# A new order for all queues of a fused recurrent-gate and gated-convolution kernel

## The chip, the cores and the metric

The kernel runs on one core of a Trainium2 chip. A core has TensorE (PE in the profile; its weight loads are PEld), VectorE (DVE), ScalarE (ACT), GpSimd (POOL) and SyncE (SP), which here only issues transfers. Each takes its own instructions strictly in order and waits at an instruction until what it needs is there. The metric is the device time of one execution in microseconds (us); lower is better.

## The reference

Two layers, one behind the other, on `x` of 4 x 6336 x 256 in float32. The first is a gated linear recurrence, the second a gated unit whose gate is a causal convolution over five time steps.

```python
# first layer, c = 8
sig_r, sig_i = sigmoid(r_gate), sigmoid(i_gate)
a_t  = exp(c * sig_r * log(sigmoid(a_param)))
norm = sqrt(maximum(1 - a_t * a_t, 1e-6))
x_gated = norm * sig_i * x
h = a_t[:, t] * h + x_gated[:, t]            # over t; y[:, t] = h
# second layer, on y
gate = sigmoid(sum_k conv_w[k] * y shifted by 4 - k)
out  = (gate * (y @ w_val)) @ w_out
```

## The kernel before

The 25,344 rows (batch and time laid end to end) are cut into 51 windows, of 512 rows each but for two of 256 at the start and one of 256 at the end; 28 chunks hold one or two windows each. Windows 0, 1 and 2 are chunks 0, 1 and 2; chunk 3 holds windows 3 and 4, chunk 4 windows 5 and 6, and so on; windows 49 and 50 are chunks 26 and 27. Sigmoids are worked out as half of one plus a tangent (tanh), so that tanh and exp share one table of ACT.

The program is one list of words, `ORDER` (line 35 on): the loop at the end of the kernel (from `for word in ORDER.split()`) reads it word by word and calls the function that the word names, which issues its instructions. Nothing else orders them: each engine's queue is the sequence of its words in the list, and what waits for what across engines follows from the buffers. A word such as `tr.5.0@6,7` is operation `tr` on chunk 5, half 0, in banks 6 and 7 of the accumulation memory (PSUM). The operations:

| word | engine, line | on | what it does |
|---|---|---|---|
| `lr`, `li`, `lx` | SP L278 | window | load of r_gate, i_gate, x into a ring of 4 windows each (`rring`, `iring`, `xring`) |
| `ta`, `tb` | ACT L296, L299 | chunk | tangent of r, of i; frees the ring slots of `lr`, `li` |
| `tr` | PE L343 | chunk group, half | transposes of the tangent of r to channels by time |
| `ex` | ACT L359 | group, half | `a_t` by an exponential, from PSUM into `aring` |
| `sq`, `sa` | POOL L367, ACT L375 | chunk, half | `a_t` squared, into `ering` |
| `rt` | ACT L386 | batch of 1 to 3 chunks | the norm by a square root; needs another table than exp and tanh |
| `pp`, `up` | POOL L306, L318 | window | one plus the tangent of i, times x, into `uring` |
| `xp`, `uv` | PE L323, DVE L332 | window | the same product by another way, for windows 1, 2 and 6 |
| `nt`, `xg` | PE L401, DVE L408 | chunk | norm transposed back; times `uring` |
| `xt` | PE L417 | chunk | the product transposed to channels by time |
| `sc` | DVE L439 | chunk, half | the recurrence, a scan along time, into `yring`; the next chunk's scan starts from its last value |
| `cv`, `tg` | PE L451, ACT L458 | window | the convolution as 20 small matmuls, its tangent |
| `vl`, `gv` | PE L466, DVE L471 | window | `y @ w_val`; gate times value, into `tgring` |
| `ou` | PE L481 | window | times `w_out`, into PSUM |
| `cd` or `ca` | DVE L489 or ACT L491 | window | copy of the output from PSUM to `oring`, a ring of 4 windows |
| `st` | SP L502 | window | store of the output |

Words with `s_` set up constants (`s_wl` loads weights on SP, `s_wcast` casts them on POOL). Where a word needs ACT's other table, a table load (L518) goes ahead of it. Loads and stores share one queue, SP's: a store that waits for its copy holds up the loads behind it in the list. A load waits until its ring slot is free, so `lr.8` for the tangent that read window 4. A matmul into a bank waits until the bank's last reader is done.

Of the kernel before, what the change touches and what calls it, by code (L numbers as in the profile page):

```python
# [15 lines left out]
CHUNKS = [[256], [256], [512], [512, 512], [512, 512], [512, 512], [512, 512], [512, 512], [512, 512], [512, 512], [512,  # L16
    512], [512, 512], [512, 512], [512, 512], [512, 512], [512, 512], [512, 512], [512, 512], [512, 512], [512,
    512], [512, 512], [512, 512], [512, 512], [512, 512], [512, 512], [512, 512], [512], [256]]
BATCHES = [[0], [1], [2], [3, 4], [5, 6, 7], [8, 9, 10], [11, 12, 13], [14, 15, 16], [17, 18, 19], [20, 21, 22], [23, 24,
    25], [26, 27]]  # L20
# [11 lines left out]
GROUPS = [[0], [1], [2], [3, 4], [5, 6], [7, 8], [9, 10], [11], [12], [13, 14], [15, 16], [17, 18], [19, 20], [21], [22],  # L32
    [23, 24], [25], [26], [27]]
# [516 lines left out]
```

## Time and profile before

| what | us |
|---|---|
| time, median of 3 runs (lowest, highest) | 296.55 (295.05, 296.58) |
| span of the profiled execution | 294.6 |
| DVE busy: scans, 62 instructions | 106.2 |
| DVE busy: gates `gv`, 51 | 59.0 |
| DVE busy: copies `cd`, 33 | 38.3 |
| ACT busy: `ex`, 38 | 54.5 |
| ACT busy: `tg`, 51 | 49.7 |
| ACT busy: `ta`, 28, and `tb`, 28 | 47.8 and 48.0 |
| ACT busy: `rt`, 15 instructions | 44.7 |
| ACT busy: table loads, 18 | 23.1 |
| ACT busy: copies `ca`, 18 | 17.8 |
| a load or store of 512 KB, from issue to landing | 7.6 to 7.9 loads, 5.2 stores |

The span runs from the first to the last instruction of the profiled execution, and the time of a run is a little more. Busy times of engines overlap; a group's row gives its total and the mean of one instruction. The sum by engine is in the page's first part. The chain that ended last is put at 38% ACT, 23% transfers, 20% PE and 12% "issue", that is, time in which the engine on the chain waited for nothing that the profile shows.

### The profile page before, as it was taken

The numbers are of one execution on the slowest core, as the hardware profiler recorded it, in microseconds if no ns is written. First come the engines' busy times: TensorE is split into PE (matmuls) and PEld (weight loads), VectorE is DVE, ScalarE is ACT, GpSimd is POOL, SyncE is SP. The second block draws the span as 40 slices with busy tenths as digits, with TensorE's granted clock in tenths as the row PEclk, the third lists the DMA queues.
The fourth block names the chain that finished last, engine by engine and source line by source line (L and its number), as shares of the span: only waits on it lengthen the run. The fifth ranks groups of instructions, "written<-read, shape, count | busy, mean of one in ns | idle before, by whom it ended". The sixth has DMA issues, their size and how long they took to land.

```text
span 294.6 us, 6238 instructions
## 1 busy us (share of the span) xinstructions
PE 241.6 (82%) x2497; PEld 165.2 (56%) x2497; DVE 241.5 (82%) x198; ACT 277.3 (94%) x202; POOL 241.8 (82%) x161
## 2 busy tenths in 40 slices
PE   2263879778697899988969889989889998899993
PEld 1241556436464767666636647566648674767652
DVE  2000697867999899997999998999999999999981
ACT  6799999999999999999999899999999999999754
POOL 1559979999999799999997989999997999666200
PEclk9999999999999999997999999999999999999998
DMA  7999999999999999999988999999999999965336
GB/s 242 336 414 388 383 408 401 403 412 376 414 398 405 401 383 388 392 356 417 385 257 312 364 411 414 415 350 406 374 389 384 392 331 369 346 249 209 153 142 249
DMA packets 29994, 104.74 MB, mean 355 GB/s; under 512 B 3335, under 2 KB 3854, under 8 KB 29966
## 3 DMA queue, kind: packets, MB, share of 16 engines
q1 hardware_dynamic: 29952, 104.35, 92.5%
q8 instruction: 19, 0.31, 0.4%
q14 instruction: 9, 0.07, 0.1%
q10 hardware_dynamic: 14, 0.01, 0.0%
HBM read 78.39 MB, written 25.95 MB: 354 GB/s over the span
## 4 chain that ended last, share of the span: by engine, by line
ACT 38%; DMA 23%; PE 20%; issue 12%; DVE 4%; SPq 1%; ACTq 0%; DVEq 0%
DMA rring<-in_r_gate_dram 10%; DMA iring<-in_i_gate_dram 9%; ACT aring L359 7%; ACT tgring L458 7%; ACT taring L296 7%; ACT ering L386 6%; ACT tbring L299 6%; PE banks L466 5%; PE banks L481 4%; PE banks L451 4%; ACT L518 4%; DMA xring<-in_x_dram 4%; PE banks L401 2%; PE banks L417 2%; DVE tgring L471 2%
## 5 line engine op out<-in xcount | busy, mean ns | idle before, releaser
L439 DVE TENSOR_TENSOR_SCAN yring<-aring,yring,banks 128x1024 bf16<-128x1024 f32 (+5 forms) x54 | 106.2, 1991 | 2.1 <-PE banks L417 1.9
L318 POOL TENSOR_TENSOR uring<-tbring,xring 128x1024 bf16<-128x1024 bf16 (+1 forms) x48 | 100.8, 2117 | 8.2 <-DMA xring<-in_x_dram 4.8
L367 POOL TENSOR_TENSOR ering<-aring 128x1024 f32<-128x1024 f32 (+2 forms) x54 | 91.5, 1714 | 11.7 <-ACT aring L359 11.6
L451 PE MATMUL banks<-yring,diag 64*64 64x512 bf16 (+7 forms) x1080 | 62.2, 362 | 3.0 <-DVE yring L439 1.1
L471 DVE SCALAR_TENSOR_TENSOR tgring<-tgring,banks 128x1024 bf16<-128x1024 bf16 (+1 forms) x51 | 59.0, 1179 | 5.7 <-ACT tgring L458 3.6
L306 POOL TENSOR_SCALAR tbring<-tbring 128x1024 bf16<-128x1024 bf16 (+1 forms) x48 | 48.9, 1030 | 13.1 <-ACT tbring L299 11.3
L481 PE MATMUL banks<-wo,tgring 128*128 128x256 bf16 x396 | 51.2, 274 | 8.3 <-DVE tgring L471 7.5
L359 ACT ACTIVATE aring<-banks,khf 128x2048 f32<-128x2048 bf16 (+3 forms) x38 | 54.5, 1472 | 1.6 <-PE banks L343 1.5
L466 PE MATMUL banks<-yring,wv 128*128 128x512 bf16 (+4 forms) x216 | 51.1, 366 | 4.7 <-ACT tgring L458 2.2
L458 ACT ACTIVATE tgring<-banks 128x1024 bf16<-128x1024 f32 (+1 forms) x51 | 49.7, 1008 | 3.4 <-PE banks L451 3.3
L481 PEld LDWEIGHTS <-tgring 128*128 128x128 bf16 x396 | 41.5, 114 | 18.7 <-DVE tgring L471 13.6
L296 ACT ACTIVATE taring<-rring 128x2048 bf16<-128x2048 f32 (+2 forms) x28 | 47.8, 1721 | 1.9 <-DMA rring<-in_r_gate_dram 1.9
L299 ACT ACTIVATE tbring<-iring 128x2048 bf16<-128x2048 f32 (+2 forms) x28 | 48.0, 1720 | 0.6 <-DMA iring<-in_i_gate_dram 0.5
L386 ACT ACTIVATE ering<-ering 128x4096 bf16<-128x4096 f32 (+5 forms) x15 | 44.7, 3016 | 0.1
L451 PEld LDWEIGHTS <-diag 64*64 64x64 bf16 x1080 | 29.0, 106 | 26.8 <-issue 10.7
L408 DVE TENSOR_TENSOR uring<-banks,uring 128x2048 bf16<-128x2048 bf16 (+2 forms) x28 | 30.3, 1095 | 15.9 <-PE banks L401 13.4
L489 DVE COPY oring<-banks 128x1024 f32<-128x1024 f32 (+1 forms) x33 | 38.3, 1183 | 5.5 <-PE banks L481 5.1
L343 PE MATMUL banks<-ident_b,taring 128*128 128x128 bf16 x396 | 30.1, 230 | 15.1 <-ACT taring L296 10.4
L343 PEld LDWEIGHTS <-taring 128*128 128x128 bf16 x396 | 26.1, 103 | 21.1 <-ACT taring L296 12.0
L466 PEld LDWEIGHTS <-wv 128*128 128x128 bf16 x216 | 19.7, 98 | 26.2 <-issue 13.1
L401 PE MATMUL banks<-ident,ering 128*128 128x128 f32 x198 | 30.0, 297 | 5.3 <-ACT ering L386 2.9
L401 PEld LDWEIGHTS banks<-ident,ering 128*128 128x128 f32 x198 | 26.9, 208 | 11.2 <-ACT ering L386 5.6
(37 smaller groups left out, 126.0 us busy)
## 6 DMA issues: line engine op xcount, KB each, us to landing
rring<-in_r_gate_dram SPq DMA_DIRECT2D x48, 512.0 KB, 7.6
iring<-in_i_gate_dram SPq DMA_DIRECT2D x48, 512.0 KB, 7.6
xring<-in_x_dram SPq DMA_DIRECT2D x48, 512.0 KB, 7.9
out_dram<-oring SPq DMA_DIRECT2D x48, 512.0 KB, 5.2
rring<-in_r_gate_dram SPq DMA_DIRECT2D x3, 256.0 KB, 3.0
iring<-in_i_gate_dram SPq DMA_DIRECT2D x3, 256.0 KB, 3.2
xring<-in_x_dram SPq DMA_DIRECT2D x3, 256.0 KB, 6.4
out_dram<-oring SPq DMA_DIRECT2D x3, 256.0 KB, 5.7
```

The lines of the kernel that those rows point to most:

```text
L296: nc.scalar.activation(**tangent(c, taring, NTR, rring, NRI))
L299: nc.scalar.activation(**tangent(c, tbring, NTI, iring, NII))
L318: nc.gpsimd.tensor_tensor(out=u, in0=t1, in1=xt, op=ALU.mult)
L359: nc.scalar.activation(out=dst, in_=src, func=ACT.Exp, scale=khf[:, h:h + 1], bias=khf[:, h:h + 1])
L367: nc.gpsimd.tensor_tensor(out=e, in0=a, in1=a, op=ALU.mult)
L401: nc.tensor.transpose(out=bank[:, k:k + P], in_=ering[:, e + q:e + wins[w] // 2:nq], identity=ident[:])
L439: nc.vector.tensor_tensor_scan(out=yring[:, h, col:col + o1 - o0], data0=aring[:, h, a_at[c] + o0:a_at[c] + o1], data1=xT[:, o0:o1], initi ...
L451: nc.tensor.matmul(out=gp[oh * 64:oh * 64 + 64, h, a:b], lhsT=diag[half * 64:half * 64 + 64, h, k, :], rhs=yring[half * 64:half * 64 + 64, ...
L458: nc.scalar.activation(out=tgring[:, w % NTG, :, 0:wins[w]], in_=live.pop(("gp", w))[:, :, 0:wins[w]], func=ACT.Tanh, scale=0.5)
L466: nc.tensor.matmul(out=val[:, m, a:b], lhsT=wv[:, hk, m * P:(m + 1) * P], rhs=yring[:, hk, col:col + b - a], start=(hk == 0), stop=(hk == ...
L471: nc.vector.scalar_tensor_tensor(out=tgring[:, w % NTG, :, 0:wins[w]], in0=tgring[:, w % NTG, :, 0:wins[w]], scalar=1.0, in1=live.pop(("va ...
L481: nc.tensor.matmul(out=ops[:, j * D:(j + 1) * D], lhsT=gv[:, hk, j:wins[w]:J], rhs=wo[:, hk, :], start=(hk == 0), stop=(hk == H - 1))
```

## The change

Only `ORDER` differs; the lists of chunks, batches and groups are wrapped to other line lengths with the same contents, and all code behind the list stands one line lower. Both lists have 961 words, and they are the same words but for five: `ca.8`, `ca.23`, `ca.33`, `ca.34` and `ca.49` became `cd.8`, `cd.23`, `cd.33`, `cd.34` and `cd.49`. The sequence of every queue differs, and so do most bank numbers. Buffers, their sizes and the shapes of all instructions are as before. Table loads between `rt` and the other words number 18 in both.

Below are the start of the list and its end, from just ahead of `rt.10`, before and after.

```diff
-s_ident s_small s_kt s_diag lr.0 ta.0 lr.1 ta.1 li.0 tr.0.1@0 tb.0 pp.0 tr.0.0@1 ex.0.1 tr.1.0@2 tr.1.1@3 lr.2 ta.2
-ex.1.0 tr.2.1@0 ex.1.1 ex.2.1 tr.2.0@2 lr.3 lr.4 lr.5 ex.0.0 ta.3 lr.6 ta.4 li.1 tr.3.1@0,1 lx.1 tb.1 sq.2.1 sq.1.1
-sq.0.1 ex.2.0 li.2 tr.3.0@2,3 li.4 lx.0 li.3 tb.2 xp.1@4 sq.0.0 sq.1.0 sq.2.0 up.0 uv.1 lr.7 lr.8 ex.3.1 sq.4.1 ex.3.0
-sq.3.0 lr.9 lr.10 lx.2 lx.4 s_wl.2 lx.3 li.5 li.6 s_wl.1 tb.3 s_wl.3 s_wl.0 ta.5 lx.5 ta.6 lr.14 rt.0 xp.2@2,3 nt.0@4
-xg.0 xt.0@0,1 li.8 li.7 uv.2 rt.1 rt.2 nt.1@4 nt.2@5 xg.2 xg.1 pp.4 sq.3.1 sq.4.0 lx.6 rt.3 lr.11 tb.4 lr.12
-tr.5.0@6,7 ex.5.0 xt.1@5,4 li.9 lr.13 sc.0.0 sc.0.1 pp.3 up.4 lx.8 nt.3@2,3 xt.2@0,1 sc.1.0 li.10 up.3 sc.1.1 xg.3
-xt.3@2,3 tb.5 cv.1@4,5 sc.2.1 lx.7 sc.2.0 tg.1 cv.0@6,7 tg.0 tr.5.1@0,1 ex.5.1 s_wcast vl.1@4,5 sc.3.1 sc.3.0 xp.6@6,7
-vl.0@0,1 nt.4@2,3 li.12 pp.5 ta.7 lr.16 sq.5.0 sq.6.0 up.5 li.11 ta.8 pp.8 uv.6 tb.6 gv.0 ou.0.0@0 lr.15 cv.2@6,7 tg.2
...
-xg.22 ex.25.1 li.46 cv.38@6,7 tg.38 sa.25.1 tb.24 pp.45 xt.22@2,3 ou.36.0@0,1 cv.37@6,7 tg.37 st.34 st.33 st.35
-sc.21.0 cv.39@4,5 lx.43 tg.39 up.43 cd.36.0 vl.37@0,1 lx.46 sc.22.0 lx.45 gv.37 rt.10 vl.38@6,7 gv.38 ou.37.0@0,1
-ou.38.0@6,7 sc.22.1 cd.38.0 cv.40@4,5 cd.37.0 tg.40 li.48 vl.39@2,3 gv.39 st.36 nt.23@6,7 pp.46 up.45 up.46 li.47
-tb.25 pp.48 pp.47 lr.49 ta.26 lx.47 st.37 st.38 li.49 li.50 xg.23 vl.40@0,1 gv.40 nt.24@2,3 xg.24 xt.23@6,7 sc.23.1
-ou.39.0@4,5 ca.39.0 tr.27.0@0 tr.27.1@1 ex.27.1 ex.27.0 lx.50 lx.48 cv.42@2,3 up.47 tg.42 st.39 cv.41@4,5 tg.41
-sc.23.0 up.48 ou.40.0@0,1 ca.40.0 st.40 sa.27.1 vl.41@2,3 gv.41 vl.42@4,5 gv.42 tr.26.1@6 sq.27.0 tr.26.0@7 ex.26.0
-xt.24@0,1 sc.24.0 ex.26.1 sq.26.1 sc.24.1 tb.26 pp.49 sq.26.0 ou.41.0@2,3 ca.41.0 cv.43@4,5 cv.44@6,7 vl.43@2,3 tg.43
-ou.42.0@4,5 tg.44 rt.11 st.41 lx.49 nt.25@6,7 ca.42.0 gv.43 vl.44@0,1 xg.25 ou.43.0@2,3 xt.25@6,7 ca.43.0 gv.44
-cv.46@4,5 tb.27 tg.46 cv.45@2,3 tg.45 sc.25.1 sc.25.0 st.42 ou.44.0@0,1 ca.44.0 nt.26@7 st.43 st.44 up.49 xg.26
-vl.46@4,5 gv.46 vl.45@2,3 gv.45 cv.47@0,1 tg.47 ou.46.0@4,5 ca.46.0 xt.26@6,7 sc.26.0 ou.45.0@0,1 vl.47@2,3 ca.45.0
-st.45 nt.27@4 cv.48@5,6 tg.48 sc.26.1 cv.49@0,1 tg.49 gv.47 pp.50 up.50 xg.27 xt.27@5,4 sc.27.1 vl.49@2,3 ou.47.0@6,7
-ca.47.0 st.46 vl.48@0,1 gv.49 ou.49.0@2,3 ca.49.0 sc.27.0 st.47 cv.50@6,7 tg.50 gv.48 st.49 ou.48.0@0,1 ca.48.0 st.48
-vl.50@2,3 gv.50 ou.50.0@2 ca.50.0 st.50
+s_ident s_small s_kt s_diag lx.1 lr.1 lr.2 lr.0 ta.0 li.0 s_wl.1 lr.3 li.1 ta.1 lr.4 tr.1.0@0 tr.0.1@1 tb.0 tr.0.0@2
+lr.5 ta.2 ex.0.1 lr.6 tr.2.1@3 ex.1.0 ex.2.1 sq.0.1 sq.1.0 xp.1@4 tr.2.0@5 lx.0 lx.3 li.4 s_wl.3 li.3 li.2 lx.2
+tr.1.1@0 ta.3 ex.2.0 s_wl.0 sq.2.0 pp.0 sq.2.1 ta.4 up.0 ex.1.1 tr.3.1@6,7 ex.0.0 lr.8 s_wl.2 sq.1.1 sq.0.0 tb.1
+tr.3.0@0,1 ex.3.1 ex.3.0 uv.1 tb.3 xp.2@6,7 sq.3.1 sq.4.1 tb.2 li.5 lr.10 uv.2 sq.3.0 li.6 lr.9 li.7 lr.7 sq.4.0
+lx.4 li.8 lx.6 rt.2 lx.5 rt.0 rt.1 pp.3 up.3 s_wcast pp.4 nt.2@6 xg.2 rt.3 nt.1@7 nt.0@0 xg.0 xg.1 xt.0@0,1 sc.0.0
+sc.0.1 xt.1@6,7 sc.1.0 sc.1.1 xt.2@4,5 cv.0@0,1 vl.0@6,7 cv.1@2,3 sc.2.1 tg.0 vl.1@0,1 gv.0 lx.7 ta.5 up.4 sc.2.0
+tg.1 ta.6 nt.3@6,7 ou.0.0@5 gv.1 tb.4 cd.0.0 ou.1.0@0 xg.3 st.0 lr.14 tr.5.1@4,5 cd.1.0 xt.3@6,7 st.1 ex.5.1 lr.12
+pp.5 cv.2@0,1 sc.3.0 lr.11 vl.2@2,3 li.10 lr.13 li.9 tg.2 tr.5.0@4,5 sc.3.1 tb.5 up.5 li.12 lx.8 xp.6@0,1 sq.6.1
...
+sq.23.0 pp.43 sq.24.1 sq.25.0 tg.38 ex.25.1 xt.22@6,7 sc.21.1 sc.21.0 tg.37 ou.36.0@4,5 tb.24 sa.25.1 vl.38@0,1
+cd.36.0 cv.39@2,3 gv.38 st.36 lx.46 li.48 tg.39 sc.22.0 li.50 ou.38.0@0,1 vl.39@4,5 vl.37@2,3 pp.46 pp.44 rt.10
+up.44 up.43 cd.38.0 up.46 gv.37 ou.37.0@2,3 pp.45 cv.40@0,1 sc.22.1 st.38 lr.49 li.47 li.49 lr.50 cv.41@6,7 gv.39
+cd.37.0 nt.23@4,5 st.37 lx.48 vl.41@2,3 up.45 tg.41 xg.23 tg.40 vl.40@6,7 gv.41 nt.24@4,5 gv.40 xt.23@2,3
+ou.41.0@0,1 lx.50 lx.47 ta.26 tb.25 ta.27 pp.47 pp.48 up.47 xg.24 ou.39.0@6,7 ca.41.0 cv.42@4,5 sc.23.1 ca.39.0
+st.41 ou.40.0@0,1 st.39 tg.42 ca.40.0 vl.42@6,7 tr.27.0@3 ex.27.0 xt.24@4,5 tb.26 st.40 sc.23.0 tr.26.0@3 gv.42
+cv.44@0,1 pp.49 ex.26.0 lx.49 ou.42.0@6,7 tr.26.1@3 tg.44 sc.24.1 tr.27.1@2 ca.42.0 ex.26.1 sc.24.0 cv.43@0,1
+nt.25@6,7 sq.26.0 up.48 xg.25 ex.27.1 sq.27.0 up.49 vl.43@2,3 tg.43 sa.27.1 tb.27 cv.45@4,5 pp.50 sq.26.1 gv.43
+tg.45 st.42 vl.45@6,7 gv.45 vl.44@0,1 xt.25@4,5 gv.44 ou.45.0@6,7 rt.11 up.50 sc.25.1 ou.44.0@0,1 ca.45.0 ca.44.0
+st.45 ou.43.0@2,3 ca.43.0 nt.26@6 st.44 sc.25.0 vl.46@0,1 cv.46@2,3 st.43 nt.27@7 tg.46 xg.26 xg.27 cv.48@4,5
+xt.26@2,3 gv.46 tg.48 cv.47@6,7 tg.47 ou.46.0@4,5 sc.26.0 sc.26.1 vl.47@0,1 ca.46.0 gv.47 st.46 vl.48@6,7 xt.27@4,5
+cv.49@2,3 vl.49@0,1 gv.48 tg.49 sc.27.0 ou.48.0@6,7 gv.49 ou.47.0@2,3 sc.27.1 ca.48.0 ou.49.0@0,1 st.48 ca.47.0
+cv.50@4,5 cd.49.0 st.47 vl.50@2,3 tg.50 gv.50 ou.50.0@2 st.49 ca.50.0 st.50
```

Some sequences of single queues that the prediction uses, read off the two lists:

| queue | before | after |
|---|---|---|
| SP, first loads | `lr.0 lr.1 li.0 lr.2 lr.3 lr.4 lr.5` | `lx.1 lr.1 lr.2 lr.0 li.0 s_wl.1 lr.3 li.1 lr.4 lr.5` |
| ACT, first | `ta.0 ta.1 tb.0 ex.0.1 ta.2 ex.1.0 ex.1.1 ex.2.1` | `ta.0 ta.1 tb.0 ta.2 ex.0.1 ex.1.0 ex.2.1 ta.3` |
| ACT, from `rt.11` | `rt.11 ca.42 ca.43 tb.27 tg.46 tg.45 ca.44 tg.47 ca.46 ca.45 tg.48 tg.49 ca.47 ca.49 tg.50 ca.48 ca.50` | `rt.11 ca.45 ca.44 ca.43 tg.46 tg.48 tg.47 ca.46 tg.49 ca.48 ca.47 tg.50 ca.50` |

More of the change, by code (lines that the diff above doesn't have):

```diff
@@ L14 @@
 ALU = mybir.AluOpType
[L16 to L20, printed above, removed]
+CHUNKS = [[256], [256], [512], [512, 512], [512, 512], [512, 512], [512, 512], [512, 512], [512, 512], [512, 512],
+    [512, 512], [512, 512], [512, 512], [512, 512], [512, 512], [512, 512], [512, 512], [512, 512], [512, 512],
+    [512, 512], [512, 512], [512, 512], [512, 512], [512, 512], [512, 512], [512, 512], [512], [256]]
+BATCHES = [[0], [1], [2], [3, 4], [5, 6, 7], [8, 9, 10], [11, 12, 13], [14, 15, 16], [17, 18, 19], [20, 21, 22],
+    [23, 24, 25], [26, 27]]
 NA = 5120
@@ L31 @@
 NOSB = 4
[L32 to L33 removed]
+GROUPS = [[0], [1], [2], [3, 4], [5, 6], [7, 8], [9, 10], [11], [12], [13, 14], [15, 16], [17, 18], [19, 20], [21],
+    [22], [23, 24], [25], [26], [27]]
 ORDER = """
[L36 to L37 removed]
@@ new lines @@
+li.31 lx.29 pp.28 tg.21 tg.22 ta.17 vl.22@2,3 nt.14@4,5 gv.21 cv.23@6,7 up.28 up.27 tb.16 gv.22 tr.17.1@0,1 xg.14
+ou.22.0@2,3 cd.22.0 tg.23 pp.29 ex.17.1 pp.30 up.29 vl.23@4,5 xt.14@6,7 gv.23 lr.38 lr.36 lr.35 st.22 lr.37
+ou.21.0@2,3 nt.15@4,5 tb.17 sc.14.1 tr.17.0@0,1 ca.21.0 st.21 cv.24@2,3 lx.31 sq.17.1 pp.32 xg.15 lx.30 sc.14.0
+ex.17.0 ou.23.0@4,5 vl.24@0,1 tg.24 xt.15@2,3 cv.26@6,7 cd.23.0 cv.25@4,5 gv.24 st.23 ta.19 ta.20 lr.39 lr.40
+sc.15.0 li.34 li.33 lr.42 tr.19.0@0,1 sq.18.0 sq.18.1 pp.31 up.30 tg.26 tg.25 vl.25@6,7 sc.15.1 nt.16@4,5 ex.19.0
```

78 lines of the change are left out of this document (37 added, 41 removed).

## The prediction

> **What bounds the kernel now.** I read the page first (busy shares and slices), then sums over chosen windows, then the waits of each engine, then the timeline of the first and last microseconds. Operations are named as in the order string: `ta.3` is the tangent of chunk 3, `rt.10` the square root of batch 10, and so on.
>
> ```profile
> span 294.6 us, 6238 instructions
> PE 241.6 (82%) x2497; PEld 165.2 (56%) x2497; DVE 241.5 (82%) x198; ACT 277.3 (94%) x202; POOL 241.8 (82%) x161
> ...
> DVE  2000697867999899997999998999999999999981
> ACT  6799999999999999999999899999999999999754
> ...
> GB/s 242 336 414 388 383 408 401 403 412 376 414 398 405 401 383 388 392 356 417 385 257 312 364 411 414 415 350 406 374 389 384 392 331 369 346 249 209 153 142 249
> DMA packets 29994, 104.74 MB, mean 355 GB/s; under 512 B 3335, under 2 KB 3854, under 8 KB 29966
> ```
>
> ScalarE (ACT) works 277.3 of 294.6 us. Its 17.3 us of idling lie at the two ends: 4.4 before 20 us, 7.0 between 260 us and its last copy at 291.7, 2.9 behind that while the last store lands; in the 240 us between there are 3.0. So ACT sets the pace of the body. The windows say who comes next:
>
> ```profile
> core 0: us, PE busy (x) PEld busy (x) DVE busy (x) ACT busy (x) POOL busy (x), PEclk, DMA share, GB/s
> 15.00:246.00 231.00, 194.79 (x2024) 133.39 (x2025) 199.17 (x159) 228.08 (x152) 216.39 (x134) 0.99 1.00 384
> 61.50:246.00 184.50, 161.34 (x1722) 112.17 (x1723) 172.37 (x131) 181.66 (x121) 175.59 (x106) 0.99 0.99 379
> 187.80:245.90 58.10, 52.82 (x583) 36.93 (x582) 56.59 (x45) 57.98 (x42) 56.39 (x35) 1.00 0.99 375
> 245.90:268.20 22.30, 21.18 (x219) 14.79 (x220) 22.25 (x16) 21.64 (x20) 16.68 (x12) 1.00 0.85 317
> 268.20:294.60 26.40, 21.95 (x231) 14.39 (x230) 18.44 (x18) 17.10 (x18) 3.94 (x3) 0.96 0.45 179
> ```
>
> The cuts are the starts of `rt.4` (61.5), `rt.8` (187.8), `rt.10` (245.9) and `rt.11` (268.2). VectorE (DVE) idles 12.1 us in the 184.5 of the second row, but only 1.5 in the third and 0.05 in the fourth: late in the body it is as full as ACT. Behind `rt.11` PE is the busiest (21.95 of 26.4).
>
> **The change, part by part.** All engines keep their operations, but five output copies go from ACT to DVE (windows 8, 23, 33, 34 and 49). Table loads stay 18. What is left is order, in four places.
>
> *The copies.* Their rows:
>
> ```profile
> L489 DVE COPY oring<-banks 128x1024 f32<-128x1024 f32 x31 | 36.9, 1215 | 3.6 <-PE banks L481 3.2 <-issue 0.3
> ...
> L491 ACT COPY oring<-banks 128x1024 f32<-128x1024 f32 x17 | 17.3, 1021 | 3.1 <-PE banks L481 2.3 <-DMA out_dram<-oring 0.8
> ```
>
> Consecutive instructions overlap in the records, by 0.065 us on ACT (its durations add up to 291 us for 277.3 busy) and by about 0.08 on DVE, so one copy is worth 0.95 us on ACT and 1.13 on DVE. Four of the five lie ahead of `rt.10`: -3.8 us on ACT. A tangent of 256 rows (`ta.27`, 0.65) moves from ahead of `rt.10` to behind it. ACT's path to `rt.10` thus falls by 4.45 us. The fifth copy is in the tail and belongs to its sum.
>
> *The start.* Before, the first load is `lr.0`, and `ta.0` starts when the exponential table is in. After, `lx.1`, `lr.1` and `lr.2` go ahead of `lr.0`, and `ta.0` is still ACT's first tangent, with all later ones queued behind it.
>
> ```profile
> 4.19 1.28 ACT L234 ACT_TABLE_LOAD   x1
> 5.49 1.15 ACT L296 ACTIVATE taring<-rring 128x512 bf16<-128x512 f32 x2
> ...
> 7.84 1.06 ACT L296 ACTIVATE taring<-rring 128x1024 bf16<-128x1024 f32 x1 [0.23 <-DMA rring<-in_r_gate_dram]
> ```
>
> The last of these lines waits for `lr.2`, the fourth load before, which ends 1.31 MB into the stream (three of 0.26 MB and one of 0.52). After, the fourth is `lr.0`, at the same 1.31 MB. So `ta.0` starts at 7.8 instead of 5.5. I then walked ACT's new queue with the durations of before: `ta.0`, `ta.1`, `tb.0`, `ta.2` and three `ex` to 12.4; `ta.3` waits for `lr.4` (3.0 MB; 13 us) and `ta.4` for `lr.6` (4.1 MB; 15.3 us) at the 0.3 to 0.4 MB per us of these microseconds; from there nothing waits, and the four first square roots end at 33.0. Before they end at 34.7, but with `ta.5` and `ta.6` (3.8 us) already done. At equal work ACT is 33.0 + 3.8 - 34.7 = 2.1 us later. Bounds: 0 if the loads land sooner than these rows, as the table is not in before 5.5 anyhow; 3.5 if `ta.3` and `ta.4` wait a microsecond longer. I take 2.1.
>
> *The body: banks, queues, stores.* No bank wait of the new order is in this trace. ACT can gain at most the 3.0 us that it idles in the body; it waited 8.0 us in all for PE (3.3 for `tg`, 3.2 for copies, 1.5 for `ex`), so a second helping of these is the other end. I take 0, as the body is nearer to the 3.0. Behind a wait of ACT stand the next `ta` and `tb`, whose ring slots SP needs for its loads. The load and store queue is one queue, SP's, and stores hold up the loads behind them:
>
> ```profile
> SPq L502 <- DVE oring L489: 62.8, 22, 6.9
> SPq L502 <- ACT oring L491: 43.3, 14, 6.2
> ```
>
> In all 106 us of SP's time goes into such waits, yet ACT misses loads for only 2.4 us (1.9 and 0.5 in its waits): the four-deep rings cover it. Both orders issue the same 204 loads and stores and the four for the weights, and have about as many loads left at `rt.10` (9 and 8). Moved stores thus cost nothing while the rings cover them; without that cover each microsecond is one of ACT's.
>
> *DVE in the body.* Between `rt.4` and `rt.10` its queue holds 2.4 us more than before, so 172.4 + 2.4 = 174.8 busy, while ACT needs 184.4 - 3.5 = 180.9 there (0.9 of the 4.45 lies ahead of `rt.4`). DVE may then idle 6.1 us where it idled 12.1. Where a queue is fuller it waits less for its inputs (1.5 in the last 58 us), so I take this as covered; the cover is thin, and a rival below has its price.
>
> *The tail.* From the start of `rt.10` to the end of the span: 48.7 before. After, DVE has 18 instructions between `rt.10` and `rt.11` (5 scans of 2.34, 8 gates of 1.21, 3 products of 1.22, 2 copies of 1.215): 27.5, less overlaps 26.0; before it was 22.3. `rt.11` waits for this, since `tg.45`, ahead of it on ACT, and its banks do. Behind `rt.11` the new order has less left, PE 16.3 us instead of 22.0 (20 matmuls of a gate 1.2, four or eight of a value 0.9, eight of an output 0.9). The walk: square root 1.5, three copies 2.9, table 1.3, `tg.46` 1.1, `gv.46` 1.2, `sc.26` 2.5, `gv.47` and `gv.48` 2.4, `sc.27.0` 0.8, `gv.49` 1.2, `sc.27.1` 0.8, `cv.50` and `vl.50` 1.3, `gv.50` 0.8, `ou.50` 0.6, last copy 0.7, store 2.9: 22.0, against 26.4 before. Together 48.0, so -0.7. Bounds: -4.4 if DVE doesn't hold back `rt.11`, and +3.7 if the last piece keeps its 26.4.
>
> *Sum.* 294.6 - 4.45 + 2.1 - 0.7 = 291.5 us for the span. The median of the runs, 296.55, is 1.95 above the span of the profiled execution; with that, 293.5 us.
>
> **Weighed against a page.** The slices move 408 to 417 GB/s for stretches, so transfers have room above the mean of 355. The Trainium skill, page "DMA: Bandwidth & Descriptors", section "Where 436 GB/s comes from", says the opposite of room: for transfers between HBM and SBUF the HBM side binds, at about 358 GB/s. By it 104.74 MB would take an estimated 292.6 us, and no order could gain. The trace disagrees, with 417 GB/s in a slice; the measurement decides.
>
> **Rivals.**
> - *VectorE takes over.* The 12.1 us that DVE idles between `rt.4` and `rt.10` may be waits for transposes and tangents that a fuller queue doesn't shorten. It decides from 6.1 us on, and each us above is one of time. If all 12.1 stay: 293.5 + 6.0 = 299.5, slower than before. For it: the copies land on an engine with 97% in the last third, and ACT's relief is no use then. Against it: 20 us of that third held DVE and ACT both above 99%. Chance 0.30.
> - *Transfers pace the body.* By `rt.10` the new order must have moved 94.2 MB, and from 15 us on (4.4 MB by then) that is 89.8 MB in 228.6 us, 393 GB/s; before it was 384. If 389, halfway, is all that comes out, the time is 231 instead of 228.6: 295.9. For it: share 1.00 of the DMA engines. Against it: 417 GB/s in slices, and ACT's 2.4 us of waiting for loads. Chance 0.14.
> - *The tail gains fully*: its lower bound, -4.4 instead of -0.7: 289.8. PE's lighter end speaks for it, DVE's 26.0 us against. Chance 0.10.
> - *Stores block loads*: two more stops of SP of the longest kind (6.9), one uncovered, would give 300.4. Chance 0.06.
>
> **How the numbers follow.** The forecast has 0.40. Half a per cent of 296.55, 1.5 us, is about what a measurement can tell from no change. Faster: forecast and tail, 0.50. Same: transfers, 0.14. Slower: VectorE and stores, 0.36. Below 289.5 lies what only both lower bounds together give; above 300.5 only DVE's full idling plus another loss: the range is 289.5 to 300.5, and the forecast's own is 291 to 295.5.
>
> **What would show it.** `ta.0` near 7.8 us; copies on ACT 13 and on DVE 38; ACT idle under 4 us between 35 us and `rt.10`, which starts near 243.5; DVE idle near 6 us from `rt.4` to `rt.10`; about 22 us from `rt.11` to the end. I am wrong if ACT idles in the body, and DVE busy all the while says that the first rival did it; if ACT waits for `rring` or `iring` there, it was transfers or stores.

## The result and the profile after

The new order takes 300.64 us in the median of 4 runs (298.92 to 302.11), beside 295.98 (295.05 to 296.58, 4 runs) for the order before on the same chip: a ratio of 1.015, interval [1.011, 1.019]. It is slower by about 4.5 us. A ratio leaves out runs in a slower state and a median does not: three of the ten of `half_after`, one each of `loads_start` and `less_dve`, further below. The profiled execution of the new order has a span of 300.0 us, 5.4 more than the 294.6 of before.

The page of the new order, its sums and two engines by slices:

```profile
span 300.0 us, 6225 instructions
...
PE 246.0 (82%) x2471; PEld 168.9 (56%) x2497; DVE 248.0 (83%) x203; ACT 273.7 (91%) x197; POOL 241.9 (81%) x161
...
DVE  2001899845989899989999999789999899997983
ACT  3799998999899989999998997999998999998943
...
GB/s 210 337 380 370 396 319 379 416 411 393 379 387 322 364 415 413 359 405 374 389 353 414 373 341 406 391 352 356 391 369 413 304 366 376 388 332 94 213 71 245
```

ACT has 3.6 us less to do than before (273.7 for 277.3), DVE 6.5 more. All the same the span grew, so ACT idles 9 us more. Where, the windows say. These are the new order's, cut at 20 us, `rt.4` (64.2), `rt.10` (250.0) and `rt.11` (276.9):

```profile
20.00:250.00 230.00, 196.41 (x1998) 135.89 (x2017) 204.36 (x163) 221.78 (x144) 212.52 (x132) 0.97 0.99 378
64.20:250.00 185.80, 159.83 (x1672) 113.25 (x1688) 172.43 (x131) 178.87 (x116) 173.74 (x105) 0.96 0.99 377
250.00:276.90 26.90, 24.07 (x241) 16.12 (x244) 24.77 (x19) 24.95 (x23) 22.55 (x17) 1.00 0.77 296
276.90:300.00 23.10, 18.45 (x194) 11.95 (x193) 16.98 (x16) 13.68 (x15) 0.91 (x1) 0.97 0.43 172
```

The fourth busy column is ACT: 221.78 of 230.0 us, 8.2 idle. The same stretch of before, from 20 us to its own `rt.10`:

```profile
20.00:245.90 225.90, 191.26 (x1999) 130.31 (x1998) 199.07 (x159) 222.98 (x148) 214.28 (x133) 0.99 1.00 383
```

Here it is 2.9. What ACT waits for in the new order (total, number of waits, longest):

```profile
ACT taring L297 <- DMA rring<-in_r_gate_dram: 7.2, 5, 3.1
ACT tgring L459 <- PE banks L452: 5.6, 7, 2.2
ACT oring L492 <- PE banks L482: 2.3, 2, 1.4
ACT aring L360 <- PE banks L344: 1.6, 2, 0.8
ACT tbring L300 <- DMA iring<-in_i_gate_dram: 1.5, 3, 1.1
...
ACT taring L297 <- issue: 1.0, 1, 1.0
```

And before, for the same loads:

```profile
ACT taring L296 <- DMA rring<-in_r_gate_dram: 1.9, 3, 1.0
...
ACT tbring L299 <- DMA iring<-in_i_gate_dram: 0.5, 1, 0.5
```

Loads of r and i that come late: 8.7 us where before it was 2.4. The 1.0 that the view puts down to "issue" is one more of them (`ta.8`, below; its load landed 0.1 us before it began), which makes 9.7. Of the 7.2, 4.2 lie in the start; the others are single tangents in the body. Written as a ledger along ACT, from the first to the last microsecond:

| term | forecast | measured, after less before | from |
|---|---|---|---|
| start: ACT idle before 20 us | +2.1 | +2.3 | 6.7 (20 less its 13.25 busy) for 4.4 |
| ACT's work ahead of `rt.10` | -4.45 | -3.55 | busy 235.03 for 238.58 |
| ACT idle from 20 us to `rt.10` | 0 | +5.3 | 8.2 for 2.9 |
| from `rt.10` to the end | -0.7 | +1.3 | 50.0 for 48.7 |
| sum | -3.05 | +5.35 | 300.0 for 294.6 |

The start came as forecast and the tail a little worse. The body is the large item: what ACT was spared came back as idle time, and more. How far such a row can be trusted, `tail_after` shows, further below: it has the order of before up to `rt.10`, and in its trace ACT idles 3.5 us ahead of 20 us (4.4 before) and 2.2 from there to `rt.10` (2.9 before). So two executions differ by about a microsecond in a row; the body's 5.3 is well beyond that, the tail's 1.3 is not.

One of these waits in full, `ta.21`. First ACT's timeline (start, duration, in brackets the idle time ahead of it and what ended it), then SP's of the same microseconds:

```profile
177.98 2.11 ACT L360 ACTIVATE aring<-banks,khf 128x2048 f32<-128x2048 bf16 x1
182.21 1.91 ACT L297 ACTIVATE taring<-rring 128x2048 bf16<-128x2048 f32 x1 [2.12 <-DMA rring<-in_r_gate_dram]
```

```profile
173.81 0.34 SPq L503 DMA_DIRECT2D out_dram<-oring  x1
174.53 1.34 SPq L279 DMA_DIRECT2D rring<-in_r_gate_dram  x2
175.93 0.91 SPq L279 DMA_DIRECT2D iring<-in_i_gate_dram  x2
```

The second of the two loads of r at 174.53 is `lr.40`, issued at 175.5, behind `lr.39` and 1.0 us after `ta.19` had freed its slot; it landed at 182.1, 6.6 us later, and ACT stood still for the last 2.1 of these. Three other tangents wait 0.85 us or more for a load in the body: `ta.8` at 51.7 (1.05, load issued at 42.9, landed at 51.6), `ta.17` at 160.6 (0.85; 153.0 and 160.5) and `tb.22` at 229.2 (1.05; 220.9 and 229.1). These three are another case than `ta.21`: the tangents that free their slots (`ta.6`, `ta.15`, `tb.20`) had ended 3.4, 16.2 and 12.6 us before the load was issued, so the place in SP's list made them late and not the ring.

### The profile page after: what moved, and what is told of

The parts are those of the page before. It is cut to its first block, busy times and chain, and to the rows that moved or that the text cites. A ratio compares the mean times of both kernels' runs of the same rounds, so it can differ in the third digit from the quotient of the medians.

```text
span 300.0 us, 6225 instructions
## 1 busy us (share of the span) xinstructions
PE 246.0 (82%) x2471; PEld 168.9 (56%) x2497; DVE 248.0 (83%) x203; ACT 273.7 (91%) x197; POOL 241.9 (81%) x161
## 4 chain that ended last, share of the span: by engine, by line
DMA 23%; ACT 21%; PE 16%; POOL 15%; DVE 12%; issue 9%; SPq 3%; ACTq 0%; POOLq 0%; DVEq 0%
DMA iring<-in_i_gate_dram 9%; DMA rring<-in_r_gate_dram 9%; POOL uring L319 8%; DVE yring L440 6%; ACT taring L297 6%; PE banks L452 4%; DVE oring L490 4%; ACT aring L360 4%; POOL ering L368 4%; PE banks L482 3%; ACT ering L387 3%; ACT tgring L459 3%; POOL tbring L307 3%; SPq L279 3%; PE banks L467 3%
## 5 line engine op out<-in xcount | busy, mean ns | idle before, releaser
L307 POOL TENSOR_SCALAR tbring<-tbring 128x1024 bf16<-128x1024 bf16 (+1 forms) x48 | 48.9, 1028 | 11.1 <-ACT tbring L300 10.1
L467 PE MATMUL banks<-yring,wv 128*128 128x512 bf16 (+7 forms) x190 | 49.9, 370 | 9.0 <-ACT tgring L459 3.8
L459 ACT ACTIVATE tgring<-banks 128x1024 bf16<-128x1024 f32 (+1 forms) x51 | 50.1, 999 | 5.9 <-PE banks L452 5.6
L490 DVE COPY oring<-banks 128x1024 f32<-128x1024 f32 (+1 forms) x38 | 44.7, 1187 | 6.7 <-PE banks L482 5.1
L387 ACT ACTIVATE ering<-ering 128x4096 bf16<-128x4096 f32 (+5 forms) x15 | 44.7, 3017 | 0.1
L452 PEld LDWEIGHTS <-diag 64*64 64x64 bf16 x1080 | 28.4, 107 | 27.1 <-issue 11.1
L344 PE MATMUL banks<-ident_b,taring 128*128 128x128 bf16 x396 | 32.1, 238 | 11.5 <-ACT taring L297 10.6
L344 PEld LDWEIGHTS <-taring 128*128 128x128 bf16 x396 | 27.9, 108 | 18.4 <-ACT taring L297 12.7
L402 PE MATMUL banks<-ident,ering 128*128 128x128 f32 x198 | 30.7, 304 | 8.8 <-ACT ering L387 6.0
L467 PEld LDWEIGHTS <-wv 128*128 128x128 bf16 x216 | 20.2, 99 | 28.8 <-issue 15.5
```

What stands on the lines that cost most here:

```text
L307: nc.gpsimd.tensor_scalar(out=t, in0=t, scalar1=1.0, scalar2=1.0, op0=ALU.mult, op1=ALU.add)
L344: nc.tensor.transpose(out=bank[:, o:o + P], in_=taring[:, place(w, NTR), j, h * P:(h + 1) * P], identity=ident_b[:])
L452: nc.tensor.matmul(out=gp[oh * 64:oh * 64 + 64, h, a:b], lhsT=diag[half * 64:half * 64 + 64, h, k, :], rhs=yring[half * 64:half * 64 + 64, ...
L459: nc.scalar.activation(out=tgring[:, w % NTG, :, 0:wins[w]], in_=live.pop(("gp", w))[:, :, 0:wins[w]], func=ACT.Tanh, scale=0.5)
L467: nc.tensor.matmul(out=val[:, m, a:b], lhsT=wv[:, hk, m * P:(m + 1) * P], rhs=yring[:, hk, col:col + b - a], start=(hk == 0), stop=(hk == ...
```

## The experiments

Each ratio is to the order of before, run on the same chip. Unless said, only the list of words differs, and nothing else in the kernel.

**The start.** `start_back` is the new order with the first loads and tangents of before:

```diff
-s_ident s_small s_kt s_diag lx.1 lr.1 lr.2 lr.0 ta.0 li.0 s_wl.1 lr.3 li.1 ta.1 lr.4 tr.1.0@0 tr.0.1@1 tb.0
+s_ident s_small s_kt s_diag lr.0 ta.0 lr.1 li.0 lr.2 lr.3 ta.1 lx.1 s_wl.1 li.1 lr.4 tr.1.0@0 tr.0.1@1 tb.0
```

> The new order with the loads of before at the start (lr.0 first, then lr.1, li.0, lr.2, lr.3; lx.1 behind ta.1), all else as changed. Both theories hold that the late first tangent costs ACT 2.3 us (idle of ACT up to 20 us: 6.7 after, 4.4 before): 300.6 - 2.3 = 298.3. A rival says that ACT waits for loads further on anyway and takes it back: 300.6.

298.79 us, ratio 1.010 [1.0062, 1.0138]; the span is 297.9, 2.1 under the new order's. Its windows from 20 us to `rt.10`, to `rt.11` and to the end:

```profile
20.00:246.90 226.90, 194.10 (x2010) 135.29 (x2008) 203.51 (x162) 220.66 (x143) 211.94 (x131) 0.98 0.99 381
246.90:274.90 28.00, 24.77 (x248) 16.79 (x249) 25.09 (x19) 24.93 (x25) 22.22 (x16) 1.00 0.74 284
274.90:297.90 23.00, 18.31 (x190) 11.35 (x188) 16.42 (x16) 13.63 (x14) 1.06 (x1) 1.00 0.43 172
```

`ta.0` starts at 5.5 again and `rt.10` at 246.9, 3.1 earlier than in the new order. ACT is busy for 220.66 of the first 226.9 us, so it still idles 6.2 in the body with 2.3 us less work than before in that stretch, and the tail is 51.0 where it was 48.7. The time gained is 0.005 of the ratio, 1.5 us with 1.6 either way by the two intervals, so the start's 2 us fit but are not pinned down: in the trace ACT idles 1.3 less ahead of 20 us (5.5 for 6.7) and 2.0 less in the body, and the tail is 1.0 longer. Most of the loss is still there.

**The copies.** `copies_back` is the new order with the five copies on ACT again, `copies_alone` the order of before with the five on DVE; the two texts differ from their parents in five words:

```diff
-cd.8.0 ... cd.23.0 ... cd.33.0 ... cd.34.0 ... cd.49.0
+ca.8.0 ... ca.23.0 ... ca.33.0 ... ca.34.0 ... ca.49.0
```

> The new order with the five output copies back on ACT at the same places of the list. Theory L (loads come late because the new load and store queue has stores ahead of loads; ACT waits 5.3 us for loads in the body): DVE is relieved but ACT gets 3.8 us more work ahead of rt.10, of which its idling takes in a part: 300 to 304. Theory V (VectorE with five more copies sets the pace): 5 x 1.13 = 5.7 us less on its path, 295.

> The kernel before with only the engines of the five copies changed (windows 8, 23, 33, 34, 49 on DVE), order as before. Theory V: DVE was as full as ACT in the last third, so four to five copies of 1.13 us lie on its path, 296.0 + 4.5 = 300.5, the whole loss. Theory L: the copies are no cause; ACT has 3.8 us less, DVE may take back most of it: 293 to 296.5.

`copies_back` takes 304.32, ratio 1.027 [1.0232, 1.0308]: 0.012 or some 3.6 us more than the new order (1.9 to 5.2, by both intervals). `copies_alone` takes 307.51, ratio 1.0388 [1.0338, 1.0437]. In its trace ACT, whose copies went away, waits for PE:

```profile
ACT tgring L458 <- PE banks L451: 10.1, 7, 3.4
ACT oring L491 <- PE banks L481: 8.3, 6, 3.1
```

So in the new order the copies are rightly on DVE, and in the old one rightly on ACT. The two sequences are fitted to their own division of work; neither the copies nor the sequence has a price by itself.

`less_dve` asks the same from the other side: the four copies ahead of `rt.10` stay on DVE, but cost it little.

```diff
+            if w in (8, 23, 33, 34):
+                dst, src = dst[:, 0:128], src[:, 0:128]
```

> The new order, with the output copies cd of windows 8, 23, 33 and 34 cut to 128 of 1024 columns, so the rest of these windows' output is left out: some 4 us less work on DVE in the body, about what these four copies brought there. If VectorE took over as the bound (the first rival): about 296.5. If not: 300 to 301.

300.15, ratio 1.0139 [1.0107, 1.0172], where the new order has 1.015: no gain to be seen from 3.9 us less on DVE (all copies 40.8 busy for 44.7): 0.3 us, with 1.5 either way. VectorE did not take over.

**Relief for ACT and POOL.** `less_act` takes work from ACT and gives it to no one; `act_before` is the same edit in the order of before; `less_pool` does it to POOL.

```diff
-            nc.scalar.activation(out=tgring[:, w % NTG, :, 0:wins[w]], in_=live.pop(("gp", w))[:, :, 0:wins[w]],
+            n = 64 if w in (8, 23, 33, 34) else wins[w]
+            nc.scalar.activation(out=tgring[:, w % NTG, :, 0:n], in_=live.pop(("gp", w))[:, :, 0:n],
...
+            t = t[:, 0:128] if w in (8, 23, 33, 34) else t
```

> The new order, with the tangent of the gate (tg) of windows 8, 23, 33 and 34 worked out for 64 columns of each piece only, so most of these gates is left out: some 3.6 us less work on ACT in the body, nothing else changed. If ACT's work paces the body by itself, 3.6 us less: about 297. If four resources share the pace, ACT idles more and the time falls by 1.5 us or less: 299 to 300.6.

> The order of before with the tangents tg of windows 8, 23, 33 and 34 worked out for 64 columns only, so most of these gates is left out: 3.6 us less work on ACT in the body, with no work moved to another engine and no queue changed. As the prediction has it, ACT sets the pace and each us less on it is one of time: 0.988 of before, about 292.5. If transfers were already at their most in the body of before (384 GB/s, share 1.00): 0.995 or more, with new waits of ACT for rring and iring.

> The new order, with the product pp of windows 8, 23, 33 and 34 worked out for 128 elements only, so the rest of these products is left out: some 3.6 us less work on POOL in the body. If POOL paces the body (it frees the slots of x and of the tangent of i, for which the loads wait): about 297. If not: 300 to 301.

| kernel | work taken off (busy sum of the group) | us | ratio, interval |
|---|---|---|---|
| new order | | 300.64 | 1.015 [1.011, 1.019] |
| `less_act` | ACT 3.1 (`tg` 47.0 for 50.1) | 299.73 | 1.0145 [1.0122, 1.0168] |
| `less_pool` | POOL 3.0 (`pp` 45.9 for 48.9) | 300.07 | 1.0149 [1.0119, 1.018] |
| order of before | | 296.76 | 1 |
| `act_before` | ACT 2.9 (`tg` 46.8 for 49.7) | 296.09 | 0.9981 [0.995, 1.0011] |

In the new order 3.1 us less on ACT bring 0.15 us (0.0005 of 296, with some 1.4 either way from the two intervals). In the order of before 2.9 us bring 0.6, with -0.3 and 1.5 as the ends. At most half of the relief arrives in either. The waits of ACT in `less_act`, and its window from 20 us to `rt.10`:

```profile
ACT taring L297 <- DMA rring<-in_r_gate_dram: 9.3, 6, 3.5
...
ACT tbring L300 <- DMA iring<-in_i_gate_dram: 3.3, 3, 2.5
```

```profile
20.00:248.60 228.60, 194.27 (x2005) 135.66 (x2023) 204.19 (x163) 219.74 (x145) 212.16 (x132) 0.99 0.99 380
```

It waits 12.6 us for loads where the new order waits 9.7. Of these 2.9 more, 1.4 lie in the start, ahead of the first window that the edit touches, so they are no effect of it; in the body the longest wait, 2.5, is `tb.22` again. Up to `rt.10`, which starts 1.4 us earlier, ACT has 2.7 us less to do and idles 1.3 more, 0.7 of that in the start. And in `act_before`, from 20 us to its `rt.10` at 244.0:

```profile
20.00:244.00 224.00, 185.96 (x1976) 128.78 (x1998) 199.30 (x159) 219.18 (x146) 213.70 (x132) 0.98 1.00 385
```

ACT idles 4.8 us of the 224 where it idled 2.9: 1.7 of it for loads of r and i (0.5 before) and 1.8 at a copy whose place in `oring` was still being stored (0.8 before). ACT is the busiest engine there, with 98%, but a microsecond less on it is not a microsecond less of time.

**The sequence of loads and stores.** `sp_back` keeps the compute queues of the new order and gives SP the sequence of before; `eager` puts every load right behind the word that frees its slot; `start_eager` is `eager` with the start of before. A part of `eager`:

```diff
-s_ident s_small s_kt s_diag lx.1 lr.1 lr.2 lr.0 ta.0 li.0 s_wl.1 lr.3 li.1 ta.1 lr.4 tr.1.0@0 tr.0.1@1 tb.0 tr.0.0@2
+s_ident s_small s_kt s_diag lx.1 lr.1 lr.2 lr.0 ta.0 lr.4 li.0 s_wl.1 lr.3 li.1 ta.1 lr.5 tr.1.0@0 tr.0.1@1 tb.0 li.4
```

> The compute queues of the new order with the sequence of loads and stores of before (12 loads or stores go earlier where the new compute order needs them). Theory L: ACT's waiting for loads in the body falls from 5.3 us to under 1.5, and the start is that of before too (-2.3): 300.6 - 4 - 2.3 = 294.3. Theory V: only the start is gained, 298.3.

> The new order in which every load of r, i and x from the second lap of its ring on stands in the list right behind the word that frees its ring slot (where it stood later); stores and all compute queues keep their sequence. Theory L (in the new queue stores stand ahead of loads that could already go, and ACT waits 5.3 us for loads in the body): this waiting falls to about 1, 300.6 - 4.3 = 296.3. Rival (the rings are refilled as fast as the transfer engines allow, an earlier place in the queue only makes a transfer wait there): 300.6. A second rival: the loads now hold up stores, and through the output ring the copies: above 302.

> The same with the start of before as in the earlier run (lr.0 first), which was worth 1.9 us by itself. If start and late loads are separate losses: 300.6 - 1.9 - 4.3 = 294.4, below before. If the late start only hid a wait for loads, or the other way round: that of the better of the two alone, 296.3 or 298.8.

`sp_back` takes 390.85 (ratio 1.32), `eager` 315.87, ratio 1.0645 [1.0572, 1.0719], `start_eager` 315.88, ratio 1.0673 [1.06, 1.0746]. What SP waits for in `eager`:

```profile
SPq L277 <- POOL uring L317: 51.3, 25, 4.6
SPq L277 <- ACT tbring L298: 35.2, 17, 5.3
...
SPq L277 <- ACT taring L295: 29.4, 16, 6.2
```

A load placed as early as its slot allows waits at the head of SP's one queue, and the other loads stand behind it. In the new order itself SP waits mostly for copies:

```profile
SPq L503 <- DVE oring L490: 95.0, 36, 7.1
SPq L503 <- ACT oring L492: 40.4, 13, 8.1
```

That is 135 us, where before it was 106 (62.8 and 43.3); for slots of the rings (behind `ta`, `tb` and `up`) it waits 22 us, where before it was 42. So SP does stand longer at stores. But that stores hold back the loads is not shown as the cause of the loss: with each load as early as its slot allows the time is worse.

`loads_four` moves only the four loads that `ta.8`, `ta.17` and `tb.22` of the section above waited for, `loads_start` adds the start of before and puts `ta.21` behind `ex.19.1`:

```diff
-xg.3 st.0 lr.14 tr.5.1@4,5 ... lr.11 vl.2@2,3 li.10 lr.13 li.9
+xg.3 st.0 lr.14 lr.13 tr.5.1@4,5 ... lr.11 vl.2@2,3 li.10 li.9
...
-li.30 lr.32 ou.18.0@0,1 ... cd.20.0 sc.13.1 lr.31 sc.13.0
+li.30 lr.32 lr.31 ou.18.0@0,1 ... cd.20.0 sc.13.1 sc.13.0
...
-cd.32.0 st.30 st.31 lx.40 ... st.32 sc.19.1 li.41 li.42 sc.19.0
+cd.32.0 li.41 li.42 st.30 st.31 lx.40 ... st.32 sc.19.1 sc.19.0
```

> The new order with four loads moved, and nothing else: lr.13 right behind lr.14, lr.31 right behind lr.32, li.41 and li.42 ahead of st.30. Their slots are free there, and in the new order ACT's waits at ta.8, ta.17 and tb.22 (1.05, 0.85 and 1.05 us) end when they land. Theory L in its narrow form (ACT paces the body, and each wait of ACT for a late load is time): 300.6 - 2.9 = 297.7. Rival D (the waits are a symptom: other queues are at that pace anyway, or the next load is as late): 300.0 to 300.6.

> The same four loads, the start of before (worth 1.9 by itself), and ta.21, which waited 2.1 us for lr.40, one place later, behind ex.19.1. Theory L: 300.6 - 1.9 - 2.9 - 1.0 = 294.8, below before. Rival D: 298.8.

`loads_four` takes 300.89, ratio 1.0136 [1.0093, 1.018]; `loads_start` 298.79, ratio 1.0062 [1.0033, 1.0091], the best form of the new order that does all its work. The waits of ACT in the latter:

```profile
ACT tgring L458 <- PE banks L451: 6.7, 9, 2.2
ACT aring L359 <- PE banks L343: 3.9, 4, 1.5
ACT taring L296 <- DMA rring<-in_r_gate_dram: 2.8, 2, 1.6
```

The waits for r are nearly gone from the body (2.8 us, all of it in the start), and ACT waits for PE's transposes (L343) in their place: 3.9 for 1.6. ACT idles 8.0 us between 20 us and `rt.10` (228.5, 220.47 busy), as much as with the late loads. In `loads_four` a load next to a moved one comes late instead: `lr.11` holds up `ta.7` for 1.1 us. Repairing the waits that the trace names moved them, in `loads_start` to words beside the ones repaired:

```profile
179.60 2.06 ACT L359 ACTIVATE aring<-banks,khf 128x2048 f32<-128x2048 bf16 x1 [1.48 <-PE banks L343]
...
230.42 1.02 ACT L458 ACTIVATE tgring<-banks 128x1024 bf16<-128x1024 f32 x1 [1.15 <-PE banks L451]
```

The first is `ex.19.1`, just ahead of the moved `ta.21`; PE has been busy since 171.9 but for 0.2 us when it starts. The second is `tg.36`, two words of ACT behind `tb.22`; ahead of it PE waits 0.7 for DVE, and DVE 1.7 for POOL. So other engines stood right behind the late loads. Against `start_back`, `loads_start` is better by 0.004 of the ratio with 0.005 either way; the 4 us expected of the late loads would have been 0.013.

**Fewer bytes.** `half_after` and `half_before` store half of each window, `half_less` is `half_after` with the edit of `less_act` on top.

```diff
-            nc.sync.dma_start(of[wstart[w]:wstart[w] + n, :].rearrange("(p j) d -> p j d", p=P),
-                              oring[:, w % NOSB, 0:J, :])
+            nc.sync.dma_start(of[wstart[w]:wstart[w] + n, :].rearrange("(p j) d -> p j d", p=P)[:, 0:J // 2, :],
+                              oring[:, w % NOSB, 0:J // 2, :])
```

> The new order with only half of every window's rows stored (the other half of the output is left out), all waits as before: 13 MB of 104.7 less to move. If the loads are late because the transfers stand in the engines' queue (they land 6.4 to 8.7 us after issue), ACT's waits for loads in the body go away: 300.6 - 4.7, and the start stays: 296. If they are late because they are issued late, or if the waits are a symptom: 299.5 or more.

> The same on the kernel before, as the control: ACT waits for loads 0.5 us there in the body, so fewer bytes give little: 295.0 to 296. Below 293 it would mean that transfers pace the body in both orders.

> The new order with half of each window's rows not stored (that part of the output is left out) and the tangents tg of windows 8, 23, 33 and 34 worked out for 64 columns only: 3.6 us less work on ACT, as in less_act, now with 12.9 MB fewer to move, as in half_after (0.999 of before). Theory T (transfers at their most, 378 to 384 GB/s with a share of 0.99, are what ACT waits for in the new body): with fewer bytes ACT's relief pays, so 0.987 of before, some 3.6 us under half_after. Theory W (waits of the order itself, whatever the bytes): less work on ACT pays no more than it did in less_act, 0.996 to 0.999.

`half_before` 294.47, ratio 0.9928 [0.9893, 0.9964]; `half_after` 297.39, ratio 0.9989 [0.9947, 1.0031]; `half_less` 295.6, ratio 0.9958 [0.9928, 0.9988]. An eighth fewer bytes take 0.0072 off the order of before (2.1 us, with 1.1 either way) and 0.0161 off the new one (4.8 us, with 1.7 either way). On top of that, ACT's 2.9 us bring 0.0031 (0.9 us), but the two intervals overlap, so this is not told from nothing. The ratio, 0.9958, is at the edge of theory W's range, and theory T's 0.987 is outside its interval. From 20 us to `rt.10` of `half_less`:

```profile
20.00:244.50 224.50, 193.11 (x2002) 134.13 (x2022) 203.46 (x163) 219.22 (x145) 211.56 (x132) 0.96 0.94 345
```

The transfers' share is 0.94 there, and ACT idles 5.3 us all the same. So the transfers are a part of what the new body waits for, the largest single one found, but not all. A smaller store is also over sooner, so that its place in `oring` is free sooner; these runs do not tell this from the fewer bytes.

**The tail, and grafts.** `tail_after` is the order of before up to `rt.10` and the remaining words in the new sequence; `tail_before` is `start_back` up to `rt.10` and then the sequence of before; `cut_rt6` is as `tail_after`, but cut at `rt.6`. No diff is shown, as only the point of the cut differs.

> The list of before up to rt.10, and from there the remaining words in the sequence of the new order (four bank numbers changed where the two meet; the copy of window 49 on DVE as in the new order, those of 8, 23, 33 and 34 on ACT as before). From the start of rt.10 to the end before takes 48.7 us and the new order 50.0. If the tail's own sequence costs this: 296.0 + 1.3 = 297.3. If the new tail is only longer since it is entered with DVE behind: 48.0 as forecast, 295.3.

> The new order with the start of before (298.8 by itself, 51.0 us from rt.10 to the end) up to rt.10, then the remaining words in the sequence of before, copy of window 49 on ACT. If the tail's own sequence is what is longer: 298.8 - 2.3 = 296.5. If the tail is entered with DVE behind, whatever its sequence: 298.8.

> The order of before up to rt.6, then the remaining words in the sequence of the new order (no bank changed). Start, first part of the body and copies up to there are those of before. Theory 1 (only the new start and the new tail cost, the new body is as good as the old): as with the order of before up to rt.10 and the new tail, that is 1.011 and about 299.4 us. Theory 2 (the new body itself costs, since ACT waits there for late loads): ACT idles over 3 us between rt.6 and rt.10 and the time is over 300.5. Theory 3 (the new body is a gain where it is entered as before): rt.10 at 243 or earlier and 297 or less.

| kernel | us | ratio, interval | span | `rt.10` | `rt.11` |
|---|---|---|---|---|---|
| `tail_after` | 299.66 | 1.0113 [1.0079, 1.0147] | 296.4 | 244.0 | 273.4 |
| `tail_before` | 311.42 | 1.0523 [1.0463, 1.0584] | 309.2 | 255.4 | |
| `cut_rt6` | 305.09 | 1.0324 [1.0292, 1.0355] | 302.1 | 252.1 | 279.1 |

The windows of `tail_after`, from 20 us to `rt.10`, to `rt.11` and to the end:

```profile
20.00:244.00 224.00, 187.23 (x1971) 129.20 (x1992) 199.05 (x158) 221.82 (x147) 213.70 (x132) 0.98 1.01 386
244.00:273.40 29.40, 27.92 (x261) 18.06 (x264) 25.43 (x19) 24.48 (x22) 19.29 (x15) 0.94 0.69 256
273.40:296.40 23.00, 18.42 (x193) 11.87 (x193) 16.95 (x16) 13.68 (x14) 1.12 (x1) 1.00 0.43 172
```

From `rt.10` to the end it takes 52.4 us, where the tail of before takes 48.7: 23.0 behind `rt.11`, as in the new order, and 29.4 ahead of it, with PE busy for 27.9 of these. `cut_rt6` answers nothing about the body: between `rt.6` and `rt.7`, just behind the seam, it takes 31.7 us (122.7 to 154.4), where the two whole orders take 27.1 and 25.6, which I put down to the seam, 4 us or more; what the new body costs behind it can't be separated. `tail_before`, slower than both its parents, fails in the same way. Only whole orders can be compared.

## Why the prediction was wrong

It said 293.5 us and a gain of 1%; it is a loss of 1.5%, and 300.64 lies just above the range, which ended at 300.5. By its own steps:

- *The start*, +2.1: right in size. `ta.0` starts at 8.6 (forecast near 7.8), and ACT's idle time ahead of 20 us grew by 2.3. `start_back` takes 0.5% off the time, though the two intervals leave room from none to 3 us.
- *The copies*, -4.45: ACT's work ahead of `rt.10` fell by 3.55, so the size was about right, but not the value given to it. (The instructions' durations add up to 294.4 us on ACT and 254.5 on DVE, so the overlaps are 0.085 and 0.066 us and a copy is worth 0.94 and 1.15; the sum changes by less than 0.1.) The step took each microsecond off ACT's work as one off the time, because "ACT sets the pace of the body". `act_before` takes 2.9 us from ACT in the very kernel that this was read from, touches nothing else, and gains 0.6 (between -0.3 and 1.5). **This is the premise that failed**: ACT was busy for 98.7% of the body, but POOL was for 95%, DVE for 88%, and the transfers' share was 1.00. That the waits of ACT were few because all ran at the same pace, and not because the others had room, is my reading of this; no run shows it by itself.
- *The body: banks, queues, stores*, "I take 0": **the step that failed in the sum**, +5.3 us of new idle time on ACT. It lay inside the bounds given (-3.0 to +8.0), but 0 was chosen for the nearness to the 3.0 that ACT idled, which is no bound on what a new order will make it wait. The range left the upper bound out, too: 293.5 + 8.0 is 301.5. Most of it is waiting for loads of r and i, 4.8 of the 5.3: `ta.8` 1.05, `ta.17` and `ta.21` 3.0, the loads of i 1.3, less 0.5 before. So "moved stores thus cost nothing while the rings cover them" counted on a cover that was not there: the loads behind the four long waits landed 6.6 to 8.7 us after their issue, and were issued too late for that by 0.85 to 2.1 us. Being late is what the trace shows; that it is the loss is not, as repairing these loads did not bring the time back (`loads_four`, `loads_start`).
- *The tail*, -0.7: +1.3. The walk was fair (26.9 for a forecast of 26.0 up to `rt.11`, 23.1 for 22.0 behind it), each part 1 us short, as it left out the waits for banks and tangents: ACT waits 4.8 us for the convolutions behind `rt.10` (3.0 before), and DVE, forecast as full up to `rt.11`, idles 2.1 of the 26.9. PE had 18.5 us to do behind `rt.11`, not 16.3. All of this is near what two executions differ by. `tail_after` makes the new tail 3.7 us longer than the old one when it is grafted on.
- *DVE in the body*: it idles 13.4 us between `rt.4` and `rt.10` (185.80 less 172.43), not 6.1. The 174.8 us of work are not there, it is 172.4 as before, and the stretch is longer than the 180.9 forecast. (The 106.2 us given for 62 scans ahead of the prediction are those of 54; the other eight take 10.1 more.) So the condition of the first rival holds and its 299.5 is near the time; yet its mechanism is refuted: with four copies cut short on DVE the time stays (`less_dve`), and with the copies off DVE it is 3.6 us longer (`copies_back`). DVE waits too, for PE above all (7.4 us at `xg` and 5.1 at the copies, over the whole span). The marker "DVE busy all the while" rightly told against it.
- *Transfers pace the body*: the rival that comes closest. The forecast asked for 393 GB/s from 15 us on. No body with all its bytes went beyond 386 GB/s from 20 us to `rt.10`, whatever was taken from an engine, and the share of the transfers was 0.99 to 1.01 in the faster ones: 383 before, 378 after, 381 in `start_back`, 385 in `act_before`, 386 in `tail_after`. As all these move the same bytes, the rate says no more than that none was faster; that the transfers could not do more is not shown by it. An eighth of the bytes is worth 4.8 us in the new order and 2.1 in the old. But its price, 295.9, was too low, and `half_less` shows 5.3 us of idling with a share of 0.94.
- *Stores block loads*: 300.4 is near the time too, and SP waits longer for stores (95.0 us for DVE's copies, 62.8 before). But `eager`, with the loads as early as their slots allow, is 5% slower than the new order. In its broad form it is refuted; that single stores hold up single loads (`ta.17`, `tb.22`) is in the trace, and freeing them gained nothing that could be measured (`loads_four`).
- *The page weighed against*: by the Trainium skill, "DMA: Bandwidth & Descriptors", section "Where 436 GB/s comes from", the side of HBM binds at about 358 GB/s. The traces disagree with the figure over 224 us (385 in `act_before`). The page "HBM Reference" of the Trainium skill, section "Specifications (TRN2)", gives some 425 for a core that streams alone; no body here came near that, with loads and stores mixed and computing beside them. That transfers leave little room was nearer to what happened than the room read from single slices of 417.

What stays open is the cause of the 5.3 us: how they divide between the transfers and the waits that engines hand to each other. That ACT, DVE or POOL alone is not what holds the new order back is shown (`less_act`, `less_dve`, `less_pool` move the ratio by 0.0005, 0.0011 and 0.0001, each with 0.005 either way, for 3 to 4 us of work, which would be 0.010 to 0.013); that the four late loads by themselves are the cause is refuted (`loads_four`, `loads_start`). No run took work off PE, whose matmuls are busy for 196.4 us from 20 us to `rt.10` where before it was 191.3, for the same count. The granted clock of TensorE, 0.975 in the profiled run for 0.990 before, speaks against itself as the cause: of the four runs of the new order the one at 0.952 was the fastest (298.92) and the one at 0.982 the slowest (302.11). With all its work done, no order that ran beats the one before.

## What to carry to other kernels

Where three engines and the transfers are each busy for 88 to 100% of a stretch, and PE for 85%, the busiest one is not the price list: take a little work off it alone, in the kernel as it is, and see whether the time follows, before crediting a move with its full length. Here five copies of 0.95 us, given back to ACT, cost 3.6 us (1.9 to 5.2), while 2.9 us taken from it gained a fifth of that and at most half. A queue order and a division of work belong together, so half of one grafted to half of another (32%, 5%, 4%, 3% and 1% slower than before here) says little about either.

## What the runs showed of the hardware

- With one queue for loads and stores on SP, a sequence that does not follow its consumers is far worse than a few late loads: 390.85 us with the old sequence under the new compute queues, in whose trace ACT waits 38.3 us for i and 20.2 for r.
- The median load of r, i or x in the new body takes 7.4 us from issue to landing and the slowest 11.3, for the 7.7 and 11.0 of before (of the three quarters of the loads whose landing the trace has): the single transfers did not become slower.
- No body that ran moved more than 386 GB/s, although slices of 7.5 us show up to 416 and 417: in the new order's body other slices are at 304 to 359. A single slice is no guide to what a whole body reached.
